# Seven-product form for part of the first FFN product of chunks 3 to 7, with single main-phase buffers and four FFN banks from step 8

## The chip, the cores and the metric

The kernel runs on one core of one Trainium2 chip. The metric is device time in microseconds of one execution of the whole program. The core has five engines, each with its own queue of instructions, worked off in the order in which the kernel's text emits them: TensorE (PE, with its weight loads as PEld), VectorE (DVE), ScalarE (ACT), GpSimd (POOL) and SyncE (SP), which here issues the transfers between the memory of the chip (HBM) and the on-chip memory (SBUF). Matrix products land in PSUM, eight banks of 512 fp32 values in each of 128 partitions; VectorE and ScalarE take them out of it.

## The reference

All data are fp32. The first part is a delta-rule attention over 4 batches, 8 heads, 768 tokens and a head dimension of 48; its output, seen as 3072 rows of 384, goes through a feed-forward network with 2048 hidden features and a leaky ReLU whose slope differs by feature.

```python
k_n = k / (np.linalg.norm(k, axis=-1, keepdims=True) + 1e-06)
for t in range(S):
    y[:, :, t] = einsum('bhd,bhde->bhe', q[:, :, t], state)
    v_old = einsum('bhde,bhd->bhe', state, kt)
    state = state + bt * einsum('bhd,bhe->bhde', kt, vt - v_old)
x = y.transpose(0, 2, 1, 3).reshape(3072, 384)
h = x @ w_in                                    # 384 x 2048
g = np.maximum(h, 0.0) + alpha * np.minimum(h, 0.0)
out = g @ w_out                                 # 2048 x 384
```

## The kernel before, in words

**Attention.** The 768 tokens are cut into 12 chunks of 64. A step is one chunk of one pair of batches, so there are 24 steps n, two to a chunk. Within a chunk the recurrence is solved as a triangular system: products of keys (`grams`, L485) give a matrix whose 32x32 diagonal blocks are inverted for four steps at a time by elimination on VectorE (`eliminate`, L560, the products at L574 and L580), nine or so steps ahead; `place` and `between` put the inverse of the 64x64 matrix together; `solve` (L923) applies it; `outputs` and `next_state` form y and the new state. `query` (L798) is the part of y that comes from the old state; ScalarE copies it out of PSUM at L808.

**Feed-forward.** The 256 tokens of a chunk go through two products. The first (`ffn_in`, L1075) makes the 2048 features as 8 pairs of 2x128 features. A plain pair takes 6 matmuls (2 feature blocks, 3 slices of the 384 inputs) of 256 columns (L1084); ScalarE then takes ReLU(-h) (L1094) and VectorE adds the slope times it (L1096, two STT). Two PSUM banks alternate. The second product (`ffn_out_fast`, `ffn_out_faster`) is made of seven products of quarters (Strassen's form, as Winograd orders it) with operand sums of the activations from VectorE (L1038) and weight sums prepared once; both functions yield 28 parts.

From chunk 8 (`FAST_IN = 8`) the first product is in the seven-product form too (`ffn_in_fast`, L1271): in two of the three input slices and the two token halves, a pair takes two matmuls of 256 columns (L1307) and seven of 128 (L1312, L1317). Four of the seven are shared by several of the four results and go to a bank of their own (`q`, `ffn_banks[3]` for every pair but the first); ScalarE copies that bank to SBUF (L1336), GpSimd forms three sums of it (L1341), VectorE adds them to the pair's own bank p (L1346, "total"), ScalarE takes ReLU(-h) (L1351, "below") and VectorE the slope (L1355, "slope"). Sums of token halves (`token_sums`, L1258) and of weights (`input_sums`, L1221) are made by VectorE. A small planner, `Due`, emits total, below and slope a given number of parts later than their pair.

**Order of the work.** All queues are in the order of emission. The feed-forward work is one generator, `feed_forward` (L1974), that yields parts: 48 for a first product (6 a pair), 28 for a second. `weave` (L1447) mixes generators by position between 0 and 1. In the main phase, from step 6 on (L2019), each step is three bursts of attention work on TensorE with a stretch of FFN parts after each:

- `burst_a(n)` (L1493): outputs and next_state of step n-1, through_state of step n and, for n below `LATE` = 16, its query; then stretch a.
- `turn_round(n)` (L1530): the y of step n-1 is turned for the FFN (`to_ffn`), the keys of step n+9 and the queries of step n+2 are turned (`flips`), loads are issued; then stretch b.
- `burst_b(n)` (L1514): solve of step n (VectorE's u, L930), grams of step n+9 or n+10 (L503 weighs them), and two `between` products whose copies (inv and mid, L768) ScalarE makes; then stretch c, into whose first part come `placing`'s scalings (L709) and the copy of the diagonal block (L734). Below step 16 these copies are emitted with the burst; from 16 on only u is, and the copies come at position 0.1 of the stretch.

Stretches a, b, c have 12, 10, 12 FFN parts in even steps and 12, 18, 12 in odd ones (step 8 has 8, 10, 12), so that every chunk lies alike: in even steps the last 6 parts of b are pair 0 and c holds pairs 1 and 2; in odd steps a holds pairs 3 and 4, b pairs 5, 6 and 7, and c begins the second product, which goes on through the next even step's a and the first 4 parts of b. Chunk c's first product begins in step 2c+2. Elimination pieces are dealt to the stretches by `TURNS` and `PIECES_OF`.

**PSUM.** Two banks are always FFN banks. The other six are three pairs, taken in rotation by the attention (`ps_big`), or from step `LATE` = 16 two pairs and two more FFN banks (`banks(2, 2)`, L2021).

**Buffers.** Keys for the turning have three buffers (`k_early`), keys for the state two (`k_late`), queries two (`q_pad`); masks `a_t`, right-hand sides `r` and solutions `u` two each.

Of the kernel before, what the change touches and what calls it, by code (L numbers as in the profile page):

```python
# [25 lines left out]
FP32 = mybir.dt.float32  # L26
# [6 lines left out]
C = 64  # L33
# [5 lines left out]
FAST_IN = 8  # L39
# [4 lines left out]
def kernel(  # L44
# [78 lines left out]
    NKE, NKL, NQ = 3, 2, 2  # L123
    ident = const.tile([128, 128], FP32, name="ident")
# [4 lines left out]
    def early(n):  # L129

        return k_late[1] if n == NKE else k_early[n % NKE]
# [10 lines left out]

    late_keys = {}

    def late_key(n):
        return late_keys.get(n, k_late[n % NKL])
# [9 lines left out]

    def load_q(n):
        if n < N:
            fetch(q, n, q_pad[n % NQ][:, :, 0:D])
# [13 lines left out]
    def load_late(n, halves=range(2)):  # L173

        if n < N:
            c, bp = steps[n]
            for t in halves:
                src = k[2 * bp + t, :, c * C : (c + 1) * C, :]
                src = src.rearrange("(g a) p d -> a p g d", a=2)
                for a in range(2):  # L180
                    dst = k_late[n % NKL].rearrange("p (g a) d -> a p g d", a=2)
                    nc.sync.dma_start(out=dst[a][half(t ^ a), :, 0:D], in_=src[a])
# [181 lines left out]

    NE = 2
# [84 lines left out]
    def flips(n_k, n_q):  # L450
# [9 lines left out]
        if n_q < N:  # L460
            p_q = p[:, 1] if both else ps_one()
            flip(q_pad[n_q % NQ], p_q)
# [51 lines left out]
    def masked(n, p):  # L514

        a_t[n] = work.tile([128, H, C], FP32, name="a_t")
# [293 lines left out]
    def through_state(n, p=None, p_y=None):  # L810
# [8 lines left out]
        asked = query(n, p_y) if n < LATE else []  # L819
# [9 lines left out]
        r = work.tile([128, 2, G, D], FP32, name="r")  # L829
# [16 lines left out]
    def scale_first(n, engine=nc.gpsimd):  # L846
# [3 lines left out]
        rhs_[n] = work.tile([128, 2, G, D], FP32, name="r")  # L850
# [59 lines left out]
    def one_round(n, i, p):  # L910
# [4 lines left out]
        if i == 2:  # L915
            us[n] = work.tile([128, 2, G, D], FP32, name="u")
# [6 lines left out]
    def solve(n, p=None):  # L923
# [5 lines left out]
        us[n] = work.tile([128, 2, G, D], FP32, name="u")  # L929
# [269 lines left out]
    held = {}  # L1199

    def spare():

        if not held:
            held["same"] = work.tile([128, NJ, H, HB], FP32, name="same", bufs=1)
            for i in range(3):
                held[i] = work.tile([128, G, 128], FP32, name="k_t", bufs=EARLY + 1)
        return held

    def input_sum(x, h):

        def four(t):
            return t.rearrange("p h d -> p (h d)").rearrange("p (i e) -> p i e", e=128)

        if x == 0:
            flat = spare()["same"].rearrange("p j h c -> p (j h c)")
            return flat.rearrange("p (i e) -> p i e", e=128)[:, 4 * h : 4 * h + 4]
        if x == 1:
            return four(k_early[h])
        return four(k_early[2]) if h == 0 else spare()[0]

    def input_sums():  # L1221

        for h in range(2):
            own = [
                w_in[:, t].rearrange("p (i f e) -> p i f e", f=2, e=128)[:, 4 * h : 4 * h + 4]
                for t in range(2)
            ]
# [868 lines left out]
```

## Time and profile before

| what | value |
|---|---|
| median of 3 runs | 646.71 us (646.24 to 647.14) |
| the profiled execution's own time | 647.49 us |
| its span, first to last instruction | 645.7 us |
| TensorE busy | 632.9 us, 98% of the span |
| VectorE, ScalarE, GpSimd busy | 484.6, 259.1, 124.4 us |
| plain pairs (L1084) | 768 instructions, 177.8 us busy |
| granted TensorE clock | 1.00 |

A row of groups gives line, engine, operation, out<-in, shape and count, then busy time and mean duration of one, then the idle time of the engine just before them and what ended it. A row of the timeline gives start, duration, engine, line, operation, names and count; in brackets is the idle time before it and what ended that. An fp32 matmul of the kernel's text is two instructions in these rows, each with a weight load. A matmul's duration includes the time through the pipeline, so starts, not durations, give the rate.

### The profile page before, as it was taken

The page shows a single profiled execution, that of the slowest core. Times are in us where ns is not written, and L with a number is a line of the kernel's source. Part 1 is how long each engine was busy: PE and PEld are TensorE (multiplying, and loading weights), DVE is VectorE, ACT ScalarE, POOL GpSimd, SP SyncE. Part 2 cuts the span into 40 slices and gives each one's busy share as a digit, 9 for nine tenths or more (in the row PEclk, how much of TensorE's full clock was granted, in tenths as well). Part 3 has the DMA queues.
Part 4 walks back from the last instruction along what each step waited for, and adds up shares of the span by engine and source line. Part 5 has one row for each costly group of instructions (what it writes and reads, how often), then busy time and mean ns, then how long its engine had stood idle before and what let it go on. Part 6 is the DMA issues. An engine that isn't in the chain of part 4 may idle for free.

```text
span 645.7 us, 21431 instructions
## 1 busy us (share of the span) xinstructions
PE 632.9 (98%) x9177; PEld 560.9 (87%) x9177; DVE 484.6 (75%) x1170; ACT 259.1 (40%) x605; POOL 124.4 (19%) x252
## 2 busy tenths in 40 slices
PE   8899899999999999999999999999999999999997
PEld 7677777567889989989989989989999999999997
DVE  5868689978998788578678577678878578477383
ACT  6676654245553253254154144033055054042240
POOL 7277610010001000000000010000043053062350
PEclk9999999999999999999999999999999999999999
DMA  8756865013511320321210211111120210100000
GB/s 133 196 161 175 239 137 127 21 31 63 100 27 28 75 50 2 67 41 21 57 29 18 45 33 25 40 39 26 39 49 14 56 21 2 40 2 2 25 0 26
DMA packets 106799, 36.89 MB, mean 57 GB/s; under 512 B 99872, under 2 KB 103088, under 8 KB 106704
## 3 DMA queue, kind: packets, MB, share of 16 engines
q1 hardware_dynamic: 104832, 35.03, 24.8%
q8 instruction: 72, 1.18, 0.8%
q10 hardware_dynamic: 1872, 0.49, 0.4%
q14 instruction: 23, 0.19, 0.1%
HBM read 30.78 MB, written 4.72 MB: 55 GB/s over the span
## 4 chain that ended last, share of the span: by engine, by line
PE 84%; DVE 9%; ACT 2%; DMA 2%; issue 1%; POOL 1%; DVEq 0%; POOLq 0%; ACTq 0%
PE p_ffn L1084 21%; PE p_ffn L1149 17%; PE p_more L1401 8%; PE p_ffn L1127 5%; PE p_more L1317 5%; PE p_ffn L1307 3%; PE p_ffn L1401 3%; PE p_ffn L1312 2%; PE p_pair L756 2%; PE p_pair L816 2%; PE p_pair L439 2%; PE p_pair L939 2%; PE p_pair L926 2%; PE p_pair L495 1%; PE p_pair L804 1%
## 5 line engine op out<-in xcount | busy, mean ns | idle before, releaser
L1084 PE MATMUL p_ffn<-xt,w_in 128*128 128x256 f32 x768 | 177.8, 384 | 2.7 <-ACT act L1094 1.6
L1084 PEld LDWEIGHTS p_ffn<-xt,w_in 128*128 128x128 f32 x768 | 141.9, 190 | 24.0 <-ACT act L1094 2.0
L1096 DVE SCALAR_TENSOR_TENSOR act<-act,al_t,p_ffn 128x256 f32<-128x256 f32 x112 | 48.5, 474 | 22.0 <-ACT act L1094 21.9
L1094 ACT ACTIVATE act<-p_ffn 128x512 f32<-128x512 f32 x56 | 33.4, 596 | 75.3 <-PE p_ffn L1084 75.1
L1341 POOL TENSOR_TENSOR k_t<-k_t 128x128 f32<-128x128 f32 (+1 forms) x48 | 29.0, 604 | 166.4 <-ACT k_t L1336 163.9
L580 DVE TENSOR_TENSOR block<-block,prod 128x30 f32<-128x30 f32 (+9 forms) x150 | 50.0, 333 | 5.2
L574 DVE TENSOR_TENSOR prod<-block 128x30 f32<-128x30 f32 (+9 forms) x150 | 48.9, 326 | 4.2 <-POOL block L564 2.8
L428 POOL TENSOR_TENSOR beta_t<-beta_t,rec 128x8 f32<-128x8 f32 x20 | 5.1, 255 | 235.0 <-DVE rec L422 219.2
L1149 PE MATMUL p_ffn<-w_out,act 128*128 128x192 f32 x288 | 49.6, 328 | 0.0
L1149 PEld LDWEIGHTS p_ffn<-w_out,act 128*128 128x128 f32 x288 | 46.5, 190 | 0.3
L982 ACT COPY xt<-p_pair 128x384 f32<-128x384 f32 x22 | 10.4, 479 | 90.6 <-PE p_pair L978 76.9
L1341 POOL TENSOR_TENSOR block<-block 128x128 f32<-128x128 f32 (+1 forms) x48 | 28.0, 582 | 17.2 <-ACT block L1336 14.7
L1307 PE MATMUL p_ffn<-xt,w_in 128*128 128x256 f32 x96 | 28.7, 380 | 0.0
L768 ACT COPY inv<-p_pair 32x256 f32<-32x256 f32 x40 | 14.5, 361 | 24.9 <-DVE u L930 24.1
L808 ACT COPY y<-p_pair 128x384 f32<-128x384 f32 x22 | 10.5, 479 | 32.8 <-PE p_pair L804 31.2
L1169 DVE TENSOR_TENSOR o_sb<-u,p_ffn 128x192 f32<-128x192 f32 x24 | 7.9, 351 | 20.8 <-PE p_ffn L1149 20.4
L1355 DVE SCALAR_TENSOR_TENSOR act<-block,al_t,act 128x256 f32<-128x256 f32 x32 | 19.1, 637 | 5.4 <-ACT block L1351 5.4
L1355 DVE SCALAR_TENSOR_TENSOR act<-k_t,al_t,act 128x256 f32<-128x256 f32 x32 | 22.3, 735 | 0.1
L834 DVE TENSOR_TENSOR r<-v_raw,p_pair 64x192 f32<-64x192 f32 (+1 forms) x60 | 21.2, 353 | 1.1
L1401 PE MATMUL p_more<-w_out,act 128*128 128x192 f32 x128 | 21.9, 329 | 0.0
L963 DVE TENSOR_TENSOR beside<-beside,p_pair 48x384 f32<-48x384 f32 (+1 forms) x38 | 20.8, 548 | 1.1 <-PE p_pair L955 0.9
L1336 ACT COPY k_t<-p_more 128x512 f32<-128x512 f32 x16 | 9.4, 586 | 30.6 <-PE p_more L1317 25.9
(292 smaller groups left out, 1412.9 us busy)
## 6 DMA issues: line engine op xcount, KB each, us to landing
v_raw<-in_v_dram SPq DMA_DIRECT2D x48, 96.0 KB, 2.9
qp<-in_q_dram SPq DMA_DIRECT2D x48, 96.0 KB, 3.0
out_dram<-o_sb SPq DMA_DIRECT2D x90, 48.0 KB, 1.6
space_out<-in_moe_w_out_dram SPq DMA_DIRECT2D x11, 384.0 KB, 3.6
ke<-in_k_dram SPq DMA_DIRECT2D x43, 96.0 KB, 3.2
kl<-in_k_dram SPq DMA_DIRECT2D x80, 48.0 KB, 2.5
w_out<-in_moe_w_in_dram SPq DMA_DIRECT2D x6, 512.0 KB, 5.0
w_out<-in_moe_w_out_dram SPq DMA_DIRECT2D x5, 384.0 KB, 4.3
```

What stands on the lines that cost most here:

```text
L574: nc.vector.tensor_tensor(out=prod, in0=r[:, 0:j, j : j + 1].to_broadcast([128, j, n]), in1=r[:, j : j + 1, j + 1 : HB].to_broadcast([128, ...
L580: nc.vector.tensor_tensor(out=r[:, 0:j, j + 1 : HB], in0=r[:, 0:j, j + 1 : HB], in1=prod, op=ALU.add)
L1084: nc.tensor.matmul(p_h[:, i], w_in[:, t, (f + i) * 128 : (f + i + 1) * 128], xt[:, t], start=(t == 0), stop=(t == KT - 1),)
L1094: nc.scalar.activation(g, p_h, ACT.Relu, scale=-1.0)
L1096: nc.vector.scalar_tensor_tensor(out=g[:, i], in0=g[:, i], scalar=al_t[:, f + i : f + i + 1], in1=p_h[:, i], op0=ALU.mult, op1=ALU.add,)
L1127: nc.tensor.matmul(p_o[u], gs[f // 2][:, f % 2, u * 128 : (u + 1) * 128], w_out[:, f], start=(f == 0), stop=(f == FT - 1),)
L1149: nc.tensor.matmul(p, x(i), w(i), start=(i == 0), stop=(i == FP - 1))
L1307: nc.tensor.matmul(p[:, f * 256 : f * 256 + 256], w(2, f), xt[:, 2], start=True, stop=False)
L1317: nc.tensor.matmul(q[:, j], a, b, start=True, stop=True)
L1341: nc.gpsimd.tensor_tensor(out=dst, in0=a, in1=b, op=ALU.add)
L1355: nc.vector.scalar_tensor_tensor(out=g[:, f], in0=r[:, f], scalar=al_t[:, 2 * i + f : 2 * i + f + 1], in1=g[:, f], op0=ALU.mult, op1=ALU.add,)
L1401: nc.tensor.matmul(p, x(i), w(i), start=(i == 0), stop=(i == FP - 1))
```

## The change

Chunks 3 to 7 take `ffn_in_fast` in place of `ffn_in` and `ffn_out_faster` in place of `ffn_out_fast`. In them pairs 1 to 6 are in the seven-product form; pairs 0 and 7 stay plain (a new function `plain`). For these chunks the slope is multiplied in by ScalarE (two multiplies by a column) and VectorE adds the result in one operation. The pair's own bank rotates over three banks. Chunks 8 to 11 keep all eight pairs in the seven-product form.

The weight sums move from VectorE to GpSimd: those of pairs 1 to 6 are emitted after the first product of chunk 2, those of pairs 0 and 7 after the first product of chunk 7. Their room, and that for the pairs' sums and ReLUs, comes from buffers that the main phase gives up: from step 7 one `a_t`, `r`, `u` and late key buffer, from step 8 one query buffer, from step 17's keys one early key buffer; and from slots of `sums`.

`banks(2, 2)` comes at step 8 (`ASK`) in place of 16. From there the query of step n+1 is made in `burst_b(n)`, in the same pair of banks as the grams; `LATE` keeps 16 for the order of the copies. The elimination's pieces are dealt out anew.

```diff
-FAST_IN = 8
+SOME, ALL = 3, 8
+ASK = 8
+ONE = 7
+    LONE = EARLY + 1 + ONE + 1
     def early(n):
-        return k_late[1] if n == NKE else k_early[n % NKE]
+        if n == NKE:
+            return k_late[1]
+        return k_early[n % NKE if n < LONE else LONE % NKE - 1]
+    def load_next(n):
+        if n + EARLY + 1 + NKE < LONE:
+            load_early(n + EARLY + 1 + NKE)
+        if n + EARLY + 2 >= LONE:
+            load_early(n + EARLY + 2)
+    def late_pad(n):
+        return k_late[n % NKL if n < ONE else 1]
+    def query_pad(n):
+        return q_pad[n % NQ if n < ASK else 0]
+    def one_of(tiles, n):
+        return tiles[n % 2 if n < ONE else 0]
...
-        asked = query(n, p_y) if n < LATE else []
+        asked = query(n, p_y) if n < ASK else []
...
+    QUICK = range(1, FP - 1)
+    beyond_sums = sums[:, FP // 2 : FP]
+    late_pads = [x.rearrange("p h d -> p (h d)") for x in (k_late[0], masks_[1])]
...
+    GROUPS = [slice(1, 5), slice(5, 6), slice(6, 7), slice(0, FP, FP - 1)]
...
-    def input_sums():
-        for h in range(2):
+    def input_sums(which):
...
-                nc.vector.tensor_tensor(out=dst, in0=x, in1=y, op=op)
-                yield
+            nc.gpsimd.tensor_tensor(out=dst, in0=x, in1=y, op=op)
...
+    BANK = 2
     def ffn_in_fast(c):
+        t, some = beyond_sums[:, :, 0], c < ALL
+        def plain(i):
+            p, g = ffn_banks[(i + BANK) % 3].rearrange("p (f i) -> p f i", f=2), act_of(c, i)
+            for f in range(2):
+                for k in range(KT):
+                    j = 2 * i + f
+                    nc.tensor.matmul(
+                        p[:, f], w_in[:, k, j * 128 : j * 128 + 128], xt[:, k],
+                        start=(k == 0), stop=(k == KT - 1),
+                    )
+                    if (f, k) == (1, KT - 1):
+                        nc.scalar.activation(g, p, ACT.Relu, scale=-1.0)
+                        for j in range(2):
+                            nc.vector.scalar_tensor_tensor(...)
+                    due.step()
+                    yield
         def pair(i):
-            p = ffn_banks[(i, 10 - i)[c == FAST_IN] % 3]
-            q = quarter(ffn_banks[2 if i == 0 else 3])
-            z, g = terms(i), act_of(c, i)
+            p = ffn_banks[(i + BANK) % 3]
+            q = ffn_banks[(BANK + 2) % 3 if i == 0 else 3].rearrange("p (i e) -> p i e", e=128)
+            z, g = beyond_sums[:, :, 1 + i % 2], act_of(c, i)
+            r = late_pads[i % 2].rearrange("p (f i) -> p f i", f=2)
...
             def below():
                 nc.scalar.activation(r, g, ACT.Relu, scale=-1.0)
+                if some:
+                    for f in range(2):
+                        nc.scalar.mul(r[:, f], r[:, f], al_t[:, 2 * i + f : 2 * i + f + 1])
             def slope():
+                if some:
+                    nc.vector.tensor_tensor(out=g, in0=g, in1=r, op=ALU.add)
+                    return
...
+            if some:
+                due.put(PER * (i + 1) + 3, total)
+                due.put(PER * (i + 2) + {last - 1: 0}.get(i, 3), below)
+                due.put(PER * (i + 2) + {last - 1: 4}.get(i, 7), slope)
...
+        if some:
+            for at in (38, 41, 44, 47):
+                due.put(at, lambda: next(first, None))
+            for at in (7, 8, 9, 10):
+                due.put(PER * FP + at, lambda: next(rest, None))
...
         for i in range(FP):
-            yield from pair(i)
+            yield from (pair if not some or i in QUICK else plain)(i)
...
     def burst_a(n):
-            later.append(lambda: load_late(n + 1))
+            if n > ONE:
+                later.append(lambda: load_late(n))
-            y = ps_big()[:, :, 0:WY] if n < LATE else None
+            y = ps_big()[:, :, 0:WY] if n < ASK else None
     def burst_b(n):
-        asked = query(n + 1, x[:, :, 0:WY]) if n + 1 >= LATE else []
+        asked = query(n + 1, x[:, :, G * C : G * C + WY]) if n + 1 >= ASK else []
     def turn_round(n):
-        load_early(n + EARLY + 1 + NKE)
+        load_next(n)
...
     def feed_forward():
-        for c in range(2, FAST_IN):
-            yield from ffn_in(c)
-            if c < FAST_IN - 1:
-                yield from ffn_out_fast(c)
...
+        yield from ffn_in(2)
+        for which in range(3):
+            input_sums(which)
+        for i, _ in enumerate(ffn_out_fast(2)):
+            if i == FAST_PARTS - 2:
+                token_sums(SOME)
+            yield
+        for c in range(SOME, NCH):
             yield from ffn_in_fast(c)
+            if c == ALL - 1:
+                input_sums(3)
             yield from ffn_out_faster(c)
...
-        JOINED + 1: (0, 4, 7), JOINED + 2: (4, 5, 5),
+        JOINED + 1: (0, 4, 7), JOINED + 2: (4, 4, 4),
-    TURNS = [(3, 3, 4), (3, 3, 4), (4, 4, 4), (0, 5, 6)]
+    TURNS = [(6, 2, 2), (2, 2, 7), (7, 2, 2), (0, 3, 8)]
-        if n == LATE:
+        if n == ASK:
             banks(2, 2)
```

## The prediction

> **What bounds the kernel now.** I read the page's busy shares first, then the waits of TensorE in the stretch that changes, then the timeline of one attention step pair there, and last the same place in chunk 8, which already runs the seven-product form. All times are of the one profiled execution: 645.7 us span, 647.49 us own time, 0.78 us (0.12%) over the median 646.71 that I forecast against.
>
> ```profile
> PE 632.9 (98%) x9177; PEld 560.9 (87%) x9177; DVE 484.6 (75%) x1170; ACT 259.1 (40%) x605; POOL 124.4 (19%) x252
> PE 84%; DVE 9%; ACT 2%; DMA 2%; issue 1%; POOL 1%; DVEq 0%; POOLq 0%; ACTq 0%
> PE p_ffn L1084 <- DVE act L1096: 0.5, 1, 0.5
> ```
>
> The first line is the busy shares, the second the engines on the chain that ended last, the third the only wait of TensorE matmuls of half a microsecond or more between 216 and 468 us, where chunks 3 to 7 run. TensorE is the bound: whatever it need not stream is gained, and whatever holds it in that stretch is new loss, since there is no old wait to hide behind. Its granted clock is 1.00 throughout.
>
> Next the timeline of step 12, stretch c (chunk 5, pairs 1 and 2): TensorE comes out of burst_b at 324.84 us, and this is what ScalarE does.
>
> ```profile
> 324.84 5.45 PE L1084 MATMUL p_ffn<-xt,w_in 128*128 128x256 f32 x24
> 324.95 0.56 DVE L930 TENSOR_TENSOR u<-p_pair,wgt 128x384 f32<-128x384 f32 x1 [0.28 <-PE p_pair L756]
> 325.54 0.74 ACT L768 COPY inv<-p_pair 32x256 f32<-32x256 f32 x2 [1.77 <-DVE u L930]
> 326.29 0.74 ACT L768 COPY mid<-p_pair 32x256 f32<-32x256 f32 x2
> 327.06 0.51 ACT L709 ACTIVATE inv<-inverse,which 128x256 f32<-128x256 f32 x1
> 327.47 0.39 ACT L734 COPY diag<-turned 128x256 f32<-128x256 f32 x1
> 327.77 0.50 ACT L709 ACTIVATE inv<-inverse,which 128x256 f32<-128x256 f32 x1
> 328.30 0.60 ACT L1094 ACTIVATE act<-p_ffn 128x512 f32<-128x512 f32 x1
> ```
>
> ScalarE starts 0.70 us after TensorE resumed (it waits for u on VectorE) and then works off a queue until 328.3; the plain pair 1, ready at about 327.4, waits for its ReLU. Nobody minds, since a plain pair has two banks to alternate between. And the same place in chunk 8:
>
> ```profile
> 471.89 0.49 PE L1317 MATMUL p_more<-xt,w_in 128*128 128x128 f32 x2
> 473.13 0.59 ACT L1336 COPY block<-p_more 128x512 f32<-128x512 f32 x1 [1.94 <-POOL k_t L1341]
> 473.62 0.73 ACT L768 COPY inv<-p_pair 32x256 f32<-32x256 f32 x2
> 474.42 0.39 PE L1317 MATMUL p_more<-xt,w_in 128*128 128x128 f32 x2
> 482.38 0.87 DVE L1355 SCALAR_TENSOR_TENSOR act<-block,al_t,act 128x256 f32<-128x256 f32 x2
> 483.23 1.87 POOL L1341 TENSOR_TENSOR k_t<-k_t 128x128 f32<-128x128 f32 x3 [0.87 <-ACT k_t L1336]
> 483.76 1.61 DVE L1355 SCALAR_TENSOR_TENSOR act<-k_t,al_t,act 128x256 f32<-128x256 f32 x2
> ```
>
> The shared products of pair 1 start at 471.89; the copy (L1336) that empties their one bank runs before the inv copies, since from step 16 burst_b puts those off; at 474.42, 2.53 us after the first, pair 2 writes that bank again. The last three rows are for VectorE against GpSimd, below.
>
> **The change, part by part.**
>
> *Streaming saved.* Per pair six 256-column products become two of 256 and seven of 128: 1408 columns for 1536. I take starts of the same stretches with plain and with fast pairs. Pairs 1 and 2: 324.84 to the next burst at 330.21 is 5.37 us, against 471.89 to 476.94, 5.05 (the 0.33 us in which the burst's first weight load waits after a plain pair goes too): 0.32. Pairs 3 and 4: 332.42 to 337.49 is 5.07, against 478.70 to 483.65, 4.95: 0.12. Pairs 5 and 6: a plain pair is 2.54 (half of 5.07), a fast one 2.43 (484.42 to 486.84), so 0.22; pair 7 stays plain. That is 0.66 us a chunk, **-3.3 us** for five. From above: chunk 7 takes 48.27 us from its first matmul to chunk 8's (419.28 to 467.55), chunk 8 47.02 (to 514.57); six eighths of 1.25 for five chunks is 4.7. I take 3.3, since pairs 0 and 7 with their burst waits are in the 1.25.
>
> *Three rotating banks for p, in place of two.* The 0.5 us wait in the third line above goes: **-0.5**; from the other side 0. Four FFN banks from step 8 leave two pairs for attention. Every reuse is then one phase apart: turn_round takes the pairs of burst_a. In step 13 VectorE has emptied them at 337.18 (L517) and the key flip starts at 337.92. The rotation of three pairs has the same distance there, and the query leaves burst_a: 0. A total (0.69) and 0.3 more ahead of L517 would cost 0.3 us in each of steps 9, 11 and 13.
>
> *The copy of the shared bank behind the burst's copies.* This is the term that decides. For n under 16 burst_b still emits u, the inv and mid copies, and now the y copy of the moved query, at once; the stretch then begins with L709 and L734, and only as the second FFN part comes pair 1's copy, into the same queue of ScalarE. By step 12's rows the second L709 began at 327.77; in its place, 0.45 later for y (L808 is 0.48, its successor starts 0.03 earlier), the copy starts at 328.22 and ends at 328.81, 3.98 us after TensorE resumed. TensorE wants the bank at 2.53. It stands 1.45 us. The same sum from the rows of steps 8, 10 and 14 (L734's successor at 226.78, 277.80 and 378.04, resumption at 223.80, 274.76 and 375.00) gives 1.49, 1.55 and 1.55. In step 16 the copies are put off, as in chunk 8, so nothing there. **+6.0 us**. Queued behind that copy on ScalarE are L709, keep's copies and ksq, which no one needs before the next burst; behind the waiting matmul is everything on TensorE. From below: 0, if u and the copies were done before the burst ends; from above 4 x 2.0, with as much again as u (0.56) ahead of y.
>
> *ScalarE's two extra multiplies per pair* (128x256 by a column, as L709, 0.41 apart) with copy 0.59 and ReLU 0.63 make some 2.0 us of ScalarE per 2.43 us pair. In odd b the key, query and norm operations end 1.63 us after the resumption (340.53 against 338.90), the copy of pair 5 at 2.2, wanted at 2.43: covered, by 0.2 us. If that cover goes, 0.3 us in each of steps 9, 11 and 13.
>
> *The sixth pair's slope at the head of the second product.* In odd b run pairs 5, 6 and plain 7; slope(5), an add on VectorE, is emitted after burst_b's u and two L503, and the moved query puts y into the pair of banks that L503 reads, y first. The trace has no such pair in burst_b, but rows near it: inv waits for u above, and in step 7 mid waits for L963, though each reads columns of its own in a shared pair.
>
> ```profile
> 189.63 0.36 ACT L768 COPY mid<-p_pair 32x256 f32<-32x256 f32 x1 [2.73 <-DVE beside L963]
> ```
>
> So I let L503 wait for y. From TensorE's resumption: inv starts at 0.70, mid at 1.45, y at 2.2 and ends at 2.68, L503 twice 0.66, the add 0.62: 3.98. The second product comes to pair 5 after five matmuls of 0.33 (8.00 us for 48 instructions, two a matmul): 1.65. It stands 2.3 us in steps 9, 11 and 13: **+7.0**. From below, L503 not waiting: u at 0.12 takes 0.56, then 0.66 and 0.62 end at 1.96: 0.3 us each. From above 3.6 each: below(3) ends at 3.6 in odd b (copy 2.2, ReLU and multiplies 1.4), and behind it VectorE has eight operations of 0.62, a piece of 0.8, the reciprocal and plain 7's 0.9, to 10.3, where u could start at 10.2 (two fast pairs 4.86, a plain 2.54, its wait 0.33, the burst 1.77, the query 0.56, then 0.12); GpSimd's chains may add 1.1. I take 2.3, which follows the two waits shown. Steps 15 and 17 have no grams: 0, at most 0.6 each.
>
> *Covered parts.* The input sums move from VectorE (eight of about 0.69) to GpSimd, in steps 6 and 7, where it idles between two weights (26.39 us in the trace ahead of step 12's L428). A 128x512 there costs 1.3 us (L270), a 128x128 0.5: some 9 us, done before weights_of(16) is emitted behind them. Uncovered, step 7's grams would wait up to 9 us, once. The loads of keys, queries and late keys into single buffers are issued after the last reader, a stretch (5 us) or more before the next, and land in 2.5 to 3.2 us; SP's queue gets no wait that it hasn't now. 0.
>
> The sum: -3.3 - 0.5 + 6.0 + 7.0 = **+9.2**, so 655.9 us.
>
> **A rule against the change.** The two STT of L1355 take 0.87 us while GpSimd is idle (482.38) and 1.61 beside its chain (483.76), 0.74 more. The Trainium skill's page "SBUF — State Buffer", section "Who interferes with whom", says that a VectorE instruction with two SBUF inputs and a GpSimd instruction that reads SBUF exclude each other, the second blocking for the whole instruction. The trace agrees by those 0.74 us. What it does here is the third rival.
>
> **The rivals.**
> *Faster, 642.9.* Pair 1's copy isn't late: if inv and mid were copied inside burst_b, they would be done by the resumption, the copy would end before 2.53 us and the add before 1.65. Then -3.8 stands. It decides from the point where the inv copies start 1.5 us earlier than in the rows above. For it: burst_b grows by 0.56 us of query, in which u could run. Against: in all four steps u starts only after the last L756 of the burst, and inv after u.
> *Nothing measurable, 647.5.* The first stall comes, the second not, and the saving is the larger one: 6.0 - 4.7 - 0.5 = +0.8.
> *Slower still, 662.* VectorE and GpSimd exclude each other. 30 more chains meet elimination pieces, slopes and operand sums with two SBUF inputs: 30 x 0.74 = 22 us of VectorE; if a quarter ends on the path through late totals and slopes, 655.9 + 6. For it: VectorE runs without a gap from 332.5 to 340 us already. Against: in odd c and even a, into which elimination is moved, it has time (7.56 us busy of 13.5 from 256.5 us).
> *The first stall alone, 649.8.* L503 doesn't wait for y: 3 x 0.3 in place of 7.0. For it: its columns are not y's. Against: the two waits shown.
>
> **How the numbers follow.** Forecast 0.54, own range 651.5 to 659.5; first stall alone 0.13; slower still 0.13; unmeasurable 0.08; faster 0.12. 0.2% is 1.3 us, about what a measurement of this kernel can tell from no change. Slower is 0.54 + 0.13 + 0.13 = 0.80, within 0.08, faster 0.12. The range leaves out the faster case and the far half of the slowest: 645.6 to 661.
>
> **What would show it.** In steps 8, 10, 12 and 14 TensorE waits some 1.5 us at pair 2's first shared product for the copy of pair 1, which stands behind inv, mid and y; in step 16 it doesn't. Waits of 2 to 3 us within the second product's first six matmuls in steps 9, 11 and 13, for VectorE's add, with L503 right behind y. Fast pairs without a wait 2.43 us apart. I am wrong if the copy of pair 1 ends within 2.5 us of the resumption, or if TensorE waits for something else: a pair of attention banks, a load, or u.

## The result

| | before | after |
|---|---|---|
| median, lowest to highest | 646.76 us, 646.24 to 647.14 (4 runs) | 670.65 us, 665.9 to 674.9 (4 runs) |
| ratio | | 1.0368 [1.0296, 1.044] |
| profiled run: own time, span | 647.49, 645.7 us | 674.9, 672.9 us |

The change costs 3.7%. The prediction said 655.9 us with a range up to 661: slower, as it came, but by 24 us and not by 9. The four runs of after lie 9 us apart, and their mean granted clocks go with their spans: 0.997 with 664.0 us, 0.987 with 667.6, 0.984 with 669.7 and 0.980 with 672.9. The last is the profiled one.

From the page of the profile of after: busy shares, and the granted clock of TensorE in 40 slices.

```profile
PE 641.9 (95%) x9357; PEld 574.3 (85%) x9357; DVE 507.9 (75%) x1182; ACT 300.7 (45%) x695; POOL 195.5 (29%) x358
...
PEclk9989999999999998997999999999799999999999
```

TensorE is busy 95% of the span where it was 98%, its busy time grew although it streams less, and the clock row, all nines before, has dips. The waits of TensorE from 216 to 480 us, where there was one of half a microsecond:

```profile
PE p_more L1460 <- DVE act L1399: 14.4, 5, 3.8
PE p_more L1358 <- ACT sums L1377: 5.3, 5, 1.2
```

The numbers are us in total, times and the longest. L1460 is the second product, L1399 the addition of the slope; L1358 are the shared products of a pair, L1377 the copy of their bank. These are the two stalls of the prediction. One by one in TensorE's timeline, from steps 8, 9, 11, 13, 15 and 17:

```profile
229.56 0.49 PE L1358 MATMUL p_more<-xt,w_in 128*128 128x128 f32 x2 [1.23 <-ACT sums L1377]
...
255.90 0.59 PE L1460 MATMUL p_more<-w_out,act 128*128 128x192 f32 x2 [3.47 <-DVE act L1399]
...
312.25 1.01 PE L1460 MATMUL p_more<-w_out,act 128*128 128x192 f32 x2 [3.81 <-DVE act L1399]
...
369.17 1.01 PE L1460 MATMUL p_more<-w_out,act 128*128 128x192 f32 x2 [3.27 <-DVE act L1399]
...
421.99 0.59 PE L1460 MATMUL p_more<-w_out,act 128*128 128x192 f32 x2 [1.20 <-DVE act L1399]
...
472.22 1.01 PE L1460 MATMUL p_more<-w_out,act 128*128 128x192 f32 x2 [2.67 <-DVE act L1399]
```

The bank copy holds TensorE 1.23 us in steps 8, 10, 12 and 14 (286.25, 343.71 and 399.51 us read the same) and not in 16, and 0.41 us in step 9 (243.10); the slope addition holds it 3.3 to 3.8 us in steps 9, 11 and 13, but also 1.20 in step 15 and 2.67 in step 17, for which the prediction had 0 to 0.6.

The first stall in ScalarE's timeline, step 8, after TensorE's resumption at 225.64 us:

```profile
226.35 0.74 ACT L796 COPY inv<-p_pair 32x256 f32<-32x256 f32 x2 [2.23 <-DVE u L958]
227.10 0.74 ACT L796 COPY mid<-p_pair 32x256 f32<-32x256 f32 x2
227.85 0.48 ACT L836 COPY y<-p_pair 128x384 f32<-128x384 f32 x1
228.22 0.51 ACT L737 ACTIVATE inv<-inverse,which 128x256 f32<-128x256 f32 x1
228.63 0.39 ACT L762 COPY diag<-turned 128x256 f32<-128x256 f32 x1
228.93 0.58 ACT L1377 COPY sums<-p_more 128x512 f32<-128x512 f32 x1
```

inv, mid, y, the first L737, the diagonal's copy and then the bank's copy, as predicted: it lets TensorE go on 3.92 us after the resumption (predicted 3.98).

The second in VectorE's timeline, step 9, after the resumption at 250.54:

```profile
249.24 0.68 DVE L1066 TENSOR_TENSOR act<-act 128x512 f32<-128x512 f32 x1
249.84 0.68 DVE L1386 TENSOR_TENSOR act<-p_more,sums 128x512 f32<-128x512 f32 x1
250.44 0.68 DVE L1066 TENSOR_TENSOR sums<-act,sums 128x512 f32<-128x512 f32 x1
251.04 0.86 DVE L1328 SCALAR_TENSOR_TENSOR act<-act,al_t,p_ffn 128x256 f32<-128x256 f32 x2
251.82 0.55 DVE L958 TENSOR_TENSOR u<-p_pair,wgt 128x384 f32<-128x384 f32 x1
254.49 0.42 DVE L531 TENSOR_TENSOR same<-p_pair,wgt 128x256 f32<-128x256 f32 x1 [2.12 <-ACT y L836]
...
255.17 0.68 DVE L1399 TENSOR_TENSOR act<-act,a_t 128x512 f32<-128x512 f32 x1
```

L531 (the Gram weighing, L503 before) waits 2.12 us for y, as the prediction let it. But u begins 1.28 us after the resumption and not 0.12: VectorE is still busy with operand sums (L1066), a total (L1386) and the slope of plain pair 7 (L1328). In steps 11 and 13 u is 1.62 and 1.08 us behind the resumption.

### The profile page after: what moved, and what is told of

Same layout as the page of the kernel before. It is cut to its first block, busy times and chain, and to the rows that moved or that the text cites. A ratio compares the mean times of both kernels' runs of the same rounds, so it can differ in the third digit from the quotient of the medians.

```text
span 672.9 us, 22058 instructions
## 1 busy us (share of the span) xinstructions
PE 641.9 (95%) x9357; PEld 574.3 (85%) x9357; DVE 507.9 (75%) x1182; ACT 300.7 (45%) x695; POOL 195.5 (29%) x358
## 4 chain that ended last, share of the span: by engine, by line
PE 70%; DVE 15%; ACT 6%; issue 3%; DMA 3%; POOL 1%; SPq 0%; ACTq 0%; DVEq 0%; POOLq 0%
PE p_more L1460 14%; PE p_ffn L1460 11%; PE p_more L1358 6%; PE p_ffn L1155 5%; PE p_ffn L1348 4%; PE p_ffn L1112 3%; PE p_ffn L1353 3%; PE p_ffn L1177 3%; PE p_more L1348 2%; PE p_more L1321 2%; PE p_pair L844 2%; PE p_pair L467 2%; DVE act L1399 2%; PE p_more L1353 2%; PE p_pair L967 2%
## 5 line engine op out<-in xcount | busy, mean ns | idle before, releaser
L1382 POOL TENSOR_TENSOR sums<-sums 128x128 f32<-128x128 f32 x186 | 112.5, 606 | 215.6 <-ACT sums L1377 205.7
L1112 PE MATMUL p_ffn<-xt,w_in 128*128 128x256 f32 x288 | 70.4, 391 | 1.8 <-ACT act L1122 0.9
L1460 PE MATMUL p_more<-w_out,act 128*128 128x192 f32 x288 | 55.9, 341 | 14.4 <-DVE act L1399 14.4
L1460 PEld LDWEIGHTS p_more<-w_out,act 128*128 128x128 f32 x288 | 48.9, 197 | 16.3 <-DVE act L1399 15.9
L1112 PEld LDWEIGHTS p_ffn<-xt,w_in 128*128 128x128 f32 x288 | 52.6, 191 | 10.9 <-ACT act L1122 1.3
L1377 ACT COPY sums<-p_more 128x512 f32<-128x512 f32 x58 | 33.9, 584 | 56.6 <-PE p_more L1358 50.7
L1348 PE MATMUL p_ffn<-xt,w_in 128*128 128x256 f32 x160 | 47.8, 380 | 0.0
L1386 DVE TENSOR_TENSOR act<-p_ffn,sums 128x512 f32<-128x512 f32 x40 | 27.2, 680 | 11.7 <-POOL sums L1382 7.3
L1460 PE MATMUL p_ffn<-w_out,act 128*128 128x192 f32 x144 | 33.3, 387 | 0.0
L1460 PEld LDWEIGHTS p_ffn<-w_out,act 128*128 128x128 f32 x144 | 31.0, 236 | 0.0
L1358 PE MATMUL p_more<-xt,w_in 128*128 128x128 f32 x116 | 24.6, 293 | 5.3 <-ACT sums L1377 5.3
L1358 PE MATMUL p_more<-sums,ke 128*128 128x128 f32 x144 | 27.8, 275 | 0.0
L1348 PE MATMUL p_more<-xt,w_in 128*128 128x256 f32 x88 | 26.3, 380 | 0.0
L1353 PEld LDWEIGHTS p_ffn<-xt,w_in 128*128 128x128 f32 x160 | 24.1, 191 | 2.1
L1460 PE MATMUL p_more<-w_out,sums 128*128 128x192 f32 x144 | 24.9, 326 | 0.0
```

The lines of the kernel that those rows point to most:

```text
L1112: nc.tensor.matmul(p_h[:, i], w_in[:, t, (f + i) * 128 : (f + i + 1) * 128], xt[:, t], start=(t == 0), stop=(t == KT - 1),)
L1348: nc.tensor.matmul(p[:, f * 256 : f * 256 + 256], w(2, f), xt[:, 2], start=True, stop=False)
L1353: nc.tensor.matmul(p[:, j * 128 : j * 128 + 128], a, b, start=False, stop=(j > 0))
L1358: nc.tensor.matmul(q[:, j], a, b, start=True, stop=True)
L1377: nc.scalar.copy(z, q)
L1382: nc.gpsimd.tensor_tensor(out=dst, in0=a, in1=b, op=ALU.add)
```

## The experiments

Three sets of kernels were measured, each on one chip beside the kernel before, which took 647.48 us there (first four experiments), 647.58 (next four) and 647.78 (last three). Times compared with the 670.65 us of after cross from one set to another. "Add waits" are TensorE's waits for L1399, "copy waits" those for L1377, from 216 to 480 us (after: 14.4 and 5.3). "Clock loss" is the sum over windows of 1 us in that stretch of busy time times one minus the granted clock (after: 9.3 us).

### The query copy behind the Gram weighings

```diff
-        now(soon + asked + gram[:2])
+        now(soon + gram[:2] + asked)
```

> The y copy is emitted after the two gram weighings, so VectorE need not wait for it. In the changed kernel's trace the add that the second product waits for ends 5.2 us after TensorE is through burst_b of step 9; of this VectorE's wait for y is 2.1. Theory (wait for y, and a late VectorE besides): TensorE's waits in steps 9, 11 and 13 fall from 3.3 to 3.8 us to 1.2 to 1.7, those of 15 and 17 (1.2 and 2.7) stay, and where a wait falls under 2 us the half clock behind it goes too: 4 to 6 us from there, 10 to 13 us in all, some 659 us. Rival (VectorE and GpSimd exclude each other, y is only what VectorE happens to stand at): the waits fall by less than 0.7 us each and the time by less than 4 us. The waits of 1.2 us for the shared bank's copy stay by both.

Measured: 660.59 us, ratio 1.020 [1.016, 1.024]; add waits 8.0, copy waits 4.9, clock loss 0. In step 9 VectorE goes from u straight on (the last row is TensorE's):

```profile
252.32 0.55 DVE L958 TENSOR_TENSOR u<-p_pair,wgt 128x384 f32<-128x384 f32 x1
252.79 0.41 DVE L531 TENSOR_TENSOR same<-p_pair,wgt 128x256 f32<-128x256 f32 x1
...
253.45 0.68 DVE L1399 TENSOR_TENSOR act<-act,a_t 128x512 f32<-128x512 f32 x1
...
254.18 0.59 PE L1460 MATMUL p_more<-w_out,act 128*128 128x192 f32 x2 [1.26 <-DVE act L1399]
```

So L531's wait for y cost 6.4 us of add waits. 8.0 us are left, in all five odd steps, and need another cause.

### The copies of inverse, mid and query later, as from step 16

```diff
+        if n >= ASK:
+            now(soon[:1] + gram[:2])
+            return soon[1:] + asked + gram[2:] + [lambda: squares(n + EARLY + 2)]
...
-soon=0.1 if n >= LATE or ends else 0.5
+soon=0.1 if n >= ASK or ends else 0.5
```

> From step 8 burst_b emits only u and the gram weighings, and the inv, mid and y copies, keep and ksq come one by one from position 0.1 of the stretch, as the inv and mid copies do from step 16. Theory: the copy of pair 1 runs 0.9 to 1.5 us after the resumption, behind two placings alone, and the four waits of 1.2 us at pair 2 go, 4.9 us; the gram weighings no longer stand behind y, so the waits for the add fall as in the run with y after the grams, to 1.2 to 1.7 us: together 15 to 18 us less than the changed kernel's 670.65, some 654. Rival (the ScalarE queue is full anyway, 2.0 us of work per pair of 2.43, and the wait only moves to pair 3 or 5): waits of TensorE for the shared bank's copy still sum to 4 us or more between 216 and 470 us.

Measured: 655.62 us, 1.0124 [1.0087, 1.0161]; add waits 8.2, copy waits 2.6. The copy waits of the even steps are gone, which settles the first stall's cause. Those that are left (0.18 and 0.94 in step 9, 0.75 and 0.73 in steps 11 and 13) are at pairs 4 and 5. In step 9 pair 4's copy waits 2.65 us for the total of pair 2, which reads the same slot of `sums` and stands on VectorE behind the evacuations of burst_a (VectorE's reads of that burst's PSUM banks):

```profile
237.20 0.59 ACT L1377 COPY sums<-p_more 128x512 f32<-128x512 f32 x1 [2.65 <-DVE act L1386]
```

### TensorE kept busy through the add waits

```diff
+    p_first, FILL_IN = [None], {3: 5, 4: 5, 5: 5, 7: 4}
...
+                if p is p_first[0] and i == 5:
+                    for _ in range(FILL_IN.get(c, 0)):
+                        nc.tensor.matmul(idle, ident, w_in[:, 0, 0 : 512 - DM // 2], start=False, stop=False)
```

> Five matmuls of 320 columns on unused columns (four in chunk 7, none in chunk 6) stand where TensorE waits for the add, some 2.7 us of the 3.3 to 3.8 us; nothing else is changed, and they end before the add does. Theory (the granted clock halves because TensorE stood idle): no slice from 250 to 480 us has a granted clock under 0.95, the waits' ends stay where they are, and the time falls by the half clock's cost, 7 to 10 us, to 661 to 664 us, with runs closer together than 666 to 675. Rival (the clock falls for the load, not for the idle time): the clock stays at 0.93 to 0.97 there and the time within 2 us of 670.65 or above.

Measured: 665.79 us (664.66 to 666.58), 1.028 [1.0248, 1.0312], clock loss 0. The order of the real work is that of after, and so are its stalls; only the idle time is filled. The gain is 4.9 us on the median, less than the 7 to 10 expected, but the spread falls from 9 us to 1.9, and the time is the 665.9 us of after's fastest run, whose clock was 0.997. One profile without half clock would not show that the filling did it, since the same order has it in some executions and not in others; the four mean clocks of 0.995 to 0.997, against 0.980 to 0.997 in after, speak for it. The profiled run of after without its clock loss, 672.9 - 9.3 - 3.4 (the last in the first 45 us) + 2.0 outside the span, would be 662, an estimate that takes all of the loss to lie on the path. The half clock is a cost of its own, in some runs and not in others.

### All pairs plain

```diff
-            yield from (pair if not some or i in QUICK else plain)(i)
+            yield from (plain if some else pair)(i)
```

with the weight sums all behind chunk 7.

> All eight pairs of chunks 3 to 7 are plain, and the weight sums are all made after chunk 7's first product; single buffers, four FFN banks from step 8, the query in burst_b and the new dealing of the pieces stay. Theory (these parts are free, all loss comes from the fast pairs): 646 to 649 us, no wait of TensorE over 0.6 us between 216 and 470 us, granted clock 1.00 there. Rival (the rotation of two pairs, the single buffers or the query's place cost): waits for attention banks, loads or u, and over 652 us.

Measured: 649.46 us, 1.003 [1.0014, 1.0047]. Buffers, banks, the query's place and the dealing of the pieces cost 2.0 us together, and 4.0 us of that profile have no known cause: two idle times of TensorE (1.6 and 0.7 us) that it calls "issue", and a clock loss of 1.7 behind the first.

```profile
298.74 0.21 PE L784 MATMUL p_pair<-diag,right 32*32 32x32 f32 x1 [1.58 <-issue]
```

The rest of the 24 us comes with the seven-product pairs.

### GpSimd's chains left out

```diff
-                    nc.gpsimd.tensor_tensor(out=dst, in0=a, in1=b, op=ALU.add)
+                    if not some:
+                        nc.gpsimd.tensor_tensor(out=dst, in0=a, in1=b, op=ALU.add)
```

> The changed kernel without GpSimd's three additions per pair in chunks 3 to 7 (they are left out, so those pairs are summed wrongly; the copy by ScalarE, the total by VectorE and everything else stay). It asks whether VectorE is late at the ends of burst b, and so the slope(5) addition, because GpSimd's chains make VectorE's own operations long (u 1.28 us after TensorE's resumption in step 9 against 0.12 in step 8). If GpSimd's chains are the cause: VectorE's long additions (0.95 to 1.04 us) fall to 0.6 to 0.7, u lies within 0.3 us of the resumption, and the waits on the slope(5) addition in steps 9, 11 and 13 fall from 3.3 to 3.8 us to the 2.3 us that the prediction gave each, about 3.5 us in all, some 662 us; the four copy waits of 1.2 us stay. If VectorE's lateness comes from the amount of its own work (evacuations, two pair totals and slopes a pair), the waits stay within 0.3 us of 3.3 to 3.8 and the time with them, 667 to 671 us.

Measured: 665.29 us (one 664.67, one 665.91); add waits 9.9, clock loss 6.5. By step: 2.65, 3.41, 2.49, 1.03 and 0.27 for 3.47, 3.81, 3.27, 1.20 and 2.67. In step 9 u begins 0.47 us after the resumption (249.28) where it was 1.28, still late behind a total, an operand sum and this:

```profile
248.97 0.87 DVE L1328 SCALAR_TENSOR_TENSOR act<-act,al_t,p_ffn 128x256 f32<-128x256 f32 x2
249.75 0.55 DVE L958 TENSOR_TENSOR u<-p_pair,wgt 128x384 f32<-128x384 f32 x1
```

Both answers in part: VectorE's long additions of step 9 fall from 0.83 to 1.04 us to 0.64 to 0.69, and the waits by 0.2 to 0.8 in steps 9 to 15. Least falls in step 11, where u is still 1.22 us late: there the longest addition stands beside an instruction of GpSimd that is in both kernels, the select of the next block for the elimination (L592). In after it reads:

```profile
304.02 1.72 POOL L592 TENSOR_SCALAR_AFFINE_SELECT block<-block 128x1024 f32<-128x1024 f32 x1
304.54 1.73 DVE L1066 TENSOR_TENSOR act<-act 128x512 f32<-128x512 f32 x1
```

In step 17 nearly the whole wait goes. There, in after, GpSimd made `input_sums(3)` from 464.63 to 468.56, beside additions of 1.21 us:

```profile
467.51 1.05 POOL L1269 TENSOR_TENSOR w_in<-w_in,same 128x256 f32<-128x256 f32 x1
467.91 1.21 DVE L1066 TENSOR_TENSOR act<-act 128x512 f32<-128x512 f32 x1
```

Without chains before them three of its four operations were done by 417.5 us.

### The last weight sums later

```diff
-                input_sums(3)
-            yield from ffn_out_faster(c)
+            for i, _ in enumerate(ffn_out_faster(c)):
+                if c == ALL - 1 and i == 10:
+                    input_sums(3)
+                yield
```

> The changed kernel with one thing moved: the last weight sums on GpSimd (input_sums(3)) are issued ten parts into chunk 7's second product instead of ahead of it. Theory: the 2.7 us wait of step 17 came from these additions, which made VectorE's operations beside them long (slope(5) 1.21 us, the evacuations 0.89). Then that wait falls to some 1.2 us, as in step 15, the half clock after it goes too, and the other waits stay: about 2 to 3 us less than the changed kernel. Rival: step 17's wait is VectorE's queue as such (it has no Gram weighing ahead of u there): then it stays over 2 us and the time too.

Measured: 669.98 us (665.94 and 674.02); waits as in after to 0.02 us, step 17's 2.65. The edit tested nothing: on GpSimd's queue no other instruction lies between the old place and the new, so the sums still run right behind pair 6's chain (457.26 us, with the first wait of step 17 at 464.84). It serves as a second profile of after's order, and one without most of the half clock: the waits 3.46, 3.81 and 3.27 are followed by no loss, only 2.65 is, by 1.5 us; its span is 663.9.

### The second stall's causes together

```diff
-        now(soon + asked + gram[:2])
+        now(soon + gram[:2] + asked)
-            for at in (38, 41, 44, 47):
+            for at in (50, 51, 53, 54):
-                due.put(PER * (i + 2) + {last - 1: 4}.get(i, 7), slope)
+                due.put(PER * (i + 2) + {last - 1: 4, last - 2: 6}.get(i, 7), slope)
```

(and the move of `input_sums(3)`, which changes nothing). The last line puts slope(5) at part 48 where it was at 49: one part earlier, so ahead of u, and not later, as the expectations of this kernel and the next word it.

> The changed kernel with the second wait's causes taken away together: the query copy y behind the two Gram weighings, the first operand sums behind the slope(5) addition, slope(5) itself one part later than in the changed kernel's order so that nothing of burst b precedes it unevenly, and input_sums(3) ten parts later. The copies of the shared bank are as in the changed kernel. If the prediction's two stalls add up: the waits on the slope(5) addition (14.4 us in the changed kernel, 8.0 with the query copy alone moved) fall under 4 us, the copy waits stay at about 5 us, and the time is about 655 to 657 us. If slope(5) is late because VectorE as a whole is behind, moving what stands before it gains nothing more than the query copy alone: 660 us.

Measured: 649.26 us (647.21 to 649.89, 10 runs), 1.0021 [1.0009, 1.0032]; add waits none, copy waits 4.9. Some 6 to 8 us better than expected: no wait on the addition is left, where up to 4 us was allowed, and no half clock behind one.

### Both stalls

The copies later, as above, with the last two changes of the diff before.

> The changed kernel with both stalls treated: ScalarE's copies of inverse, mid and query behind the bank's copy from step 8 on, the operand sums behind the slope(5) addition, that addition one part later, input_sums(3) ten parts later. If the two stalls and the half clock behind them are the whole loss: the add waits fall from 14.4 us to under 4, the copy waits to the 2.6 us of the odd steps, and the time is 649 to 652 us, against 655.6 with the copies alone moved. The same kernel with every pair plain took 649.5 us, and streaming is worth 3.3 us less than that, so without any wait it would be about 646. If VectorE is simply behind at the end of burst b, the add waits stay near 8 us and the time near 655.

Measured: 647.26 us (644.15 to 648.57, 12 runs), 0.9995 [0.998, 1.0011]; add waits none, copy waits 2.6. That is 2 us under the expected range. With two stalls treated the change is no slower than the kernel before.

### slope(5) alone earlier

```diff
-                due.put(PER * (i + 2) + {last - 1: 4}.get(i, 7), slope)
+                due.put(PER * (i + 2) + {last - 1: 4, last - 2: 6}.get(i, 7), slope)
```

> The changed kernel with one number changed: slope(5) falls due at part 48 and not 49, so that it stands on VectorE ahead of burst b's u and its two Gram weighings, not behind them. If the second stall is the place in the queue, as predicted: in step 9 VectorE would come to the addition when it now begins u, 1.28 us after the resumption, and end it some 0.7 us later, about when the ten matmuls of 1.89 us ahead of act(5) end, so the add waits fall from 14.4 us to under 2 us, no half clock follows, the copy waits stay at about 5 us, and the time is 649 to 652 us, as with the query copy and the operand sums moved too (649.3). If the place in the queue is a part only and VectorE's load counts as much: waits of 1 us a step stay, 655 us or more.

Measured: 660.87 us, 1.0207 [1.0172, 1.0241]; add waits 7.6, clock loss 1.7. The expectation was wrong by 9 us or more. slope(5) is in time in steps 9 and 13 and 0.46 late in step 11, but next in the order comes slope(6), behind u and the wait for y:

```profile
250.65 0.68 DVE L1399 TENSOR_TENSOR act<-act,a_t 128x512 f32<-128x512 f32 x1
251.25 0.55 DVE L958 TENSOR_TENSOR u<-p_pair,wgt 128x384 f32<-128x384 f32 x1
253.93 0.42 DVE L531 TENSOR_TENSOR same<-p_pair,wgt 128x256 f32<-128x256 f32 x1 [2.13 <-ACT y L836]
...
254.60 0.68 DVE L1399 TENSOR_TENSOR act<-act,kl 128x512 f32<-128x512 f32 x1
...
255.34 0.92 PE L1460 MATMUL p_more<-w_out,act 128*128 128x192 f32 x4 [1.41 <-DVE act L1399]
```

The stall moves on to act(6), at 1.4 us in each of the three steps; step 15 keeps 0.74 and step 17 2.19.

### The operand sums alone later

```diff
-            for at in (38, 41, 44, 47):
+            for at in (50, 51, 53, 54):
```

> The changed kernel with the four operand sums of the first part (2.6 to 3.9 us of VectorE in each chunk) issued behind the slope(5) addition, at parts 50 to 54, and slope(5) left where it was, behind u and the Gram weighings. Theory: VectorE came to u 1.2 us late because of them; then u follows the resumption by 0.1 to 0.3 us, the waits of steps 9, 11 and 13 fall from 3.3 to 3.8 us to the 2.3 us of the prediction, those of steps 15 and 17, where no weighing precedes the addition, to under 0.5 us, and the add waits are 7 to 8 us in all: some 658 to 661 us. Rival: VectorE is late through GpSimd's chains and the elimination's work; then the waits of steps 9, 11 and 13 stay over 3 us and the time over 664.

Measured: 661.76 us (660.64 and 662.87), 1.0211 [1.0168, 1.0255]; add waits 6.9, copy waits 5.4, clock loss 5.1. The waits are as expected by the theory (6.9 for 7 to 8); the time lies 0.8 us above its range, and the half clock was not in it:

```profile
250.87 0.56 DVE L958 TENSOR_TENSOR u<-p_pair,wgt 128x384 f32<-128x384 f32 x1 [0.73 <-PE p_pair L784]
253.55 0.42 DVE L531 TENSOR_TENSOR same<-p_pair,wgt 128x256 f32<-128x256 f32 x1 [2.13 <-ACT y L836]
...
254.96 0.59 PE L1460 MATMUL p_more<-w_out,act 128*128 128x192 f32 x2 [2.32 <-DVE act L1399]
...
364.67 0.59 PE L1460 MATMUL p_more<-w_out,act 128*128 128x192 f32 x2 [2.32 <-DVE act L1399]
```

u begins 0.12 us after the resumption (250.75), the waits of steps 9, 11 and 13 (2.32, 2.30, 2.32) are the 2.3 us of the prediction, and steps 15 and 17 have none. The two parts of the second stall nearly add up: 6.4 us go with y moved, 7.5 with the operand sums moved, of 14.4.

### Without any wait

As "both stalls" (without `input_sums(3)`), and the total of pair 2 right behind its products:

```diff
-                due.put(PER * (i + 1) + 3, total)
+                due.put(PER * (i + 1) + {2: 0}.get(i, 3), total)
```

> The changed kernel with the copies of inverse, mid and query behind the bank's copy, the operand sums behind slope(5), slope(5) one part earlier, and the total of pair 2 issued right behind that pair's products, ahead of the evacuations of burst a: without the last this order took 647.3 us and kept copy waits of 2.6 us, which came from pair 4's copy waiting 2.65 us for that total on VectorE. If that is so, these waits fall under 0.5 us and the time to 644 to 645.5 us, under the 647.6 us of the kernel before. If the waits are only moved (VectorE now blocks on GpSimd's chain of pair 2 and is late with the evacuations of burst a): another wait of TensorE of like size appears in steps 9, 11 and 13 and the time stays at 647.

Measured: 645.03 us (642.59 to 646.98, 12 runs) against 647.78, ratio 0.9958 [0.9941, 0.9974]: 0.4% faster than the kernel before. The waits that are left from 216 to 480 us:

```profile
PE p_pair L467 <- DVE a_t L545: 0.4, 1, 0.4
PE p_more L1358 <- ACT sums L1377: 0.3, 1, 0.3
```

The first is the rival's wait (burst_a's evacuations behind the earlier total), at a sixth of the size.

## Why the prediction was right and wrong

The stretch from chunk 3's first matmul to chunk 8's, in the profiled runs, with what is known in it:

| kernel | stretch, us | add waits | copy waits | clock loss | rest |
|---|---|---|---|---|---|
| before | 248.2 | 0 | 0 | 0 | 248.2 |
| after | 273.9 | 14.4 | 5.3 | 9.3 | 244.9 |
| operand sums later | 261.8 | 6.9 | 5.4 | 5.1 | 244.4 |
| second stall's causes | 248.6 | 0 | 4.9 | 0 | 243.7 |
| both stalls | 246.0 | 0 | 2.6 | 0 | 243.4 |
| without any wait | 243.8 | 0 | 0.3, and 0.4 on L545 | 0 | 243.1 |

Ahead of it after is 1.4 us longer than before. A clock loss of 3.4 us lies in the first 45 us, but the kernel with both stalls treated has none there and still begins chunk 3 1.1 us later than before, so the cause of the 1.4 is open. From chunk 8 on they take 178.1 and 178.3 us. So 25.7 + 1.4 + 0.1 make the 27.2 us between the spans, and the rest column tells that the waits and the half clock explain after to within 1.8 us.

*Streaming, -3.3, and the third bank, -0.5: right.* The rest is 3.3 us below before in after, and 4.5 to 5.1 in the three kernels with few or no waits, for 3.8 forecast (5.2 with the upper bound); the old 0.5 us wait is gone. The stretch of the all-plain kernel, 251.5 us, less the 4.0 named above, leaves 247.5: some 0.7 of the gain comes without the seven-product pairs, the rest with them.

*The copy of the shared bank, +6.0: right.* 3.92 us from resumption to the next shared product, forecast 3.98, wanted at 2.53: 1.39 us from start to start by step 8's rows, 1.23 in the profile's count of idle time. Putting off the copies removed these four waits, which shows the cause. The queue's cover of 0.2 us for pair 5 failed by 0.41 us in step 9 alone, where 0.3 in three steps was named.

*The slope at the head of the second product, +7.0: the mechanism was right, the size was half.* L531 does wait for y, and with VectorE on time the waits are 2.30 to 2.32 us. The step that failed is "u at 0.12", on which "inv starts at 0.70" rests: the term of 2.3 us a step let VectorE reach burst_b with an empty queue. In the sum VectorE's backlog stands only in the bound from above, 3.6 us. By the diff's part numbers its "eight operations" behind below(3) are two slopes, two totals and the four operand sums at parts 38, 41, 44 and 47; the measured 3.47, 3.81 and 3.27 us lie at that bound. The choice of the lower figure was the mistake, and "Steps 15 and 17 have no grams: 0, at most 0.6 each" left the backlog out, for 1.20 and 2.67 measured. The four sums take VectorE 3.2 us in steps 9, 13 and 15, and 3.9 in steps 11 and 17 (0.88, 1.15, 1.21 and 0.67 in the last). With them u is 1.1 to 1.6 us behind the resumption in steps 9, 11 and 13, without them 0.12 in step 9, and the waits of steps 15 and 17 go: 7.5 us, shown by moving them.

*The third rival, VectorE and GpSimd excluding each other, +6:* there, but as part of the above, since with the operand sums moved the same chains cause no lateness. Leaving out the chains took 4.5 us off the add waits, 2.4 of it in step 17, where the long additions stand mostly beside the weight sums, which the prediction had costed at nothing because GpSimd idles. They were hidden on GpSimd and paid for by VectorE beside it. This part is argued from the rows: no run moved the weight sums alone. An addition of two SBUF inputs took 0.68 us alone, up to 1.21 beside GpSimd's additions and 1.73 beside its select. The Trainium skill's "SBUF — State Buffer", "Who interferes with whom", has this rule; these rows agree.

*What had no term at all: the clock.* Some add waits come with several us at half the granted clock, in which a dozen matmuls of the second product take 3.79 us in place of some 2. Windows of 2 us, with the busy time of PE, PEld, DVE, ACT and POOL, the clock and the DMA share; first after, behind the wait that ended at 255.90:

```profile
254.00:256.00 2.00, 0.10 (x1) 0.10 (x1) 1.51 (x4) 1.90 (x5) 0.00 (x0) 1.00 0.00 0
256.00:258.00 2.00, 2.00 (x8) 2.00 (x9) 1.90 (x6) 0.10 (x1) 0.00 (x0) 0.63 0.00 0
258.00:260.00 2.00, 2.00 (x8) 2.00 (x8) 1.93 (x6) 0.00 (x0) 0.00 (x0) 0.51 0.00 0
```

and the kernel with the last weight sums later, behind the same wait, which ended at 254.68:

```profile
253.00:255.00 2.00, 0.32 (x2) 0.32 (x3) 1.73 (x4) 1.77 (x5) 0.00 (x0) 1.00 0.00 0
255.00:257.00 2.00, 2.00 (x14) 2.00 (x13) 1.90 (x6) 0.00 (x0) 0.00 (x0) 1.00 0.00 0
```

8 matmuls in 2 us in one, 14 in the other. This added 9.3 us to the profiled run and makes the runs of after scatter by 9 us; the three reordered kernels without add waits have none of it in this stretch.

So of the 27.2 us between the profiled spans, some 9 are what was forecast, 7.4 the add waits above 7.0, 9.3 the clock, and 1.4 lie ahead of the stretch. The direction was right by its two stalls; the size failed by the term of the second and by the missing clock. What stays open: those 1.4 us, why the stretch's rest is 1.2 to 1.8 us longer with the stalls than without, why the half clock comes in some executions only, and what the "issue" times of TensorE in the all-plain kernel are.

## What to carry to other kernels

Sum up a wait on an in-order queue from the work that is emitted ahead of it on that queue in the changed kernel, not from when the engine was free in the old one: the four sums that decided half of the second stall were in the diff. A change that streams less but loses its cover can be worth its saving again by the order of a few instructions alone: 671 us became 645 with the same operations. Moving a single one of them (slope(5)) only hands the wait to the next in the queue, so follow the queue to its end before costing a mend.

## What was not expected of the hardware

- Waits of TensorE of 2.2 to 3.8 us come with half clock in some executions and not in others: after 2.3 us three times of three in the kernel with the operand sums later, after 3.3 to 3.8 us three of three in the profile of after and none of three in the profile with the same order; after the 2.65 to 2.67 us of step 17 in those two profiles and not in two other kernels. Waits for an addition or a copy of up to 1.8 us had none, but the idle time of 1.6 us that the all-plain kernel's profile calls "issue" had. The half clock lasted 3.4 or 6.8 us. The Trainium skill's "TensorE: Matmul & The Clock Gate", Part 1, tells of a free-running window of about 3.4 us, after an idle one of which the clock is halved. The 3.4 us and the scatter agree with that; that 2.3 us of waiting, and once 1.6 us of idling, can be enough does not agree with a wholly idle window.
- A VectorE read of a pair of PSUM banks waited 2.11 to 2.12 us for ScalarE's copy of other columns of that pair in each of steps 8 to 14, and not where the copy came second. The Trainium skill's "PSUM — Partial Sum Buffer", "PSUM bank collisions raise a hardware error", says that the compiler orders two engines that touch the same partition quadrant of one bank, reads included; these rows agree.
